# Where weight conversions stand in the queues of ScalarE and VectorE: behind the newest exponential, gh, x and gl

## Chip, cores and metric

One core of a Trainium2 chip runs the whole program. The metric is the device time of one execution in microseconds. The engines meant here are TensorE (PE: matrix products and transposes), ScalarE (ACT), VectorE (DVE) and SyncE (SP, which only issues DMAs). Each works through its own queue in the order in which the program was laid out, and waits on semaphores for what another engine or a DMA has to finish.

## What is computed

Attention with a window of 32 positions for 4 x 512 local queries and full attention for 4 x 32 global ones (8 heads of 64), then two feed-forward layers over the 2176 resulting rows, in float32. The weights come as float64 and are read as raw pairs of int32.

```
out_g = np.matmul(sm(s_g), v_all)                  # s_g: global queries against all keys
s_ll = np.where(mask, s_ll, -1000000000.0)         # mask: |i - j| <= 32
a_l = sm(np.concatenate([s_lg, s_ll], axis=-1))
out_l = np.matmul(a_l, np.concatenate([v_g, v_l], axis=2))
x = rows of concatenate([out_g, out_l])            # 2176 x 512
h = x @ w_in;  g = np.maximum(0.01 * h, h);  x = g @ w_out      # first layer, d_ff 2048
h = x @ w_in2; g = h - np.tanh(h);           out = g @ w_out2   # second layer
```

## The kernel before

**Precision.** Each float32 operand of a large product is split into a high part (written by ScalarE: xh, gh, woh, win) and a low remainder (written by VectorE as a difference: xl, gl, wol, win), and each product is three matmuls.

**Items.** The first layer is worked in 80 items n. An item is a chunk c of up to 512 rows (five chunks, in the order 0, 1, 0, 2, 3, 4; the first and third each with half of the 16 slices) and a slice f of 128 of the 2048 hidden columns. `mlp1_a` does 12 matmuls into the one PSUM bank h, then `mlp1_g` the PReLU g and the high part gh on ScalarE (L206, L207) and the low part gl on VectorE (L208). The next item's h can start when g has read the bank. Two items later `mlp1_b` adds the slice's contribution to four banks y0 to y3 (12 matmuls); after a chunk's last slice `mlp1_y` evicts them through the tile yst (ScalarE L255 for y1 and y3, VectorE L257 for y0 and y2). TensorE's order for this part is written out by hand.

**Attention beside it.** The rest of the attention is worked in stages between the steps of items 0 to 7, 24 to 31, 32 to 47 and 48 to 58. A stage transposes keys and queries (kps, qps, copied to kt, qt by ScalarE), forms scores (sps), takes row minima (VectorE L418 or L412), exponentials e (ScalarE L425), their reciprocal sums and products (VectorE L434, L435, L444), transposes of the probabilities (ptps, copied to pt), and the product with v (avps), whose high part xh ScalarE writes (L485) and whose low part xl VectorE writes (L487). For global queries there are sgps, gtps, gt2ps and gavps. In the run phase all these share three PSUM banks in rotation, so that a transpose can wait for the xl that still has to read the bank.

**Weight conversions.** `convert_w` turns a raw tile (128 x 512 float64) into float32: ScalarE scales the upper words (L128, into wf or w2f), VectorE puts bits together in three steps (L129, L133, L136). First-layer weights are then split (ScalarE L142, VectorE L143) and, for w_out, stored to DRAM (wod); second-layer weights are stored as they are (w2id, w2od) through the tile w2f, which has two buffers. Raw tiles (wraw) have two buffers also; `job_load` issues the load of the next one when a conversion gives its buffer back. `job` is traced at the start of an item: in items 17 to 24 each item has one first-layer conversion, and every second item one of the second layer too; later there is about one second-layer conversion in two items.

**What sets the order.** The scheduler lays out each engine's queue by priority and by when it expects operands. `tc.issue_after(x)` adds an order edge behind instruction x, for instructions on x's engine alone. Before the change first-layer conversions stood behind the newest exponential (ScalarE) and the newest xl (VectorE), second-layer ones behind the newest gl (VectorE) and nothing on ScalarE.

Of the kernel before, what the change touches and what calls it, by code (L numbers as in the profile page):

```python
# [10 lines left out]
AF = mybir.ActivationFunctionType  # L11
# [10 lines left out]
def kernel(  # L22
# [14 lines left out]
    nc = tc.nc  # L37
# [57 lines left out]
    def f32(t):  # L95
        return t.bitcast(F32)
# [21 lines left out]
    def convert_w(raw, w=None):  # L118
        hw, lw = raw[:, :, 1], raw[:, :, 0]
        t = mlp.tile([128, DM], I32, tag="wt", name="wt", bufs=1)  # L120
        if w is None:
            w = mlp.tile([128, DM], F32, tag="wf", name="wf", bufs=2)
        nw[0] += 1

        nc.scalar.activation(w, hw.bitcast(F32), AF.Copy, scale=REBIAS)  # L128
        nc.vector.tensor_scalar(  # L129
            out=t, in0=w.bitcast(I32), scalar1=3, scalar2=0x7FFFFFFF,  # L130
            op0=ALU.logical_shift_left, op1=ALU.bitwise_and,
        )
        nc.vector.scalar_tensor_tensor(  # L133
            out=t, in0=hw, scalar=-0x80000000, in1=t, op0=ALU.bitwise_and, op1=ALU.bitwise_or
        )
        nc.vector.scalar_tensor_tensor(  # L136
            out=w.bitcast(I32), in0=lw, scalar=29, in1=t, op0=ALU.logical_shift_right, op1=ALU.bitwise_or
        )
        return w
# [10 lines left out]
    def wo_split(f, w):  # L150
        hi = mlp.tile([128, DM], F32R, tag="woh", name="woh", bufs=4)
        lo = mlp.tile([128, DM], F32R, tag="wol", name="wol", bufs=3)
        split_w(w, hi, lo, nc.vector)
        wo_t[f] = hi, lo
# [8 lines left out]

    g_t = {}
    y_ps = {}
    anchor = [None]
    last_av = [None]
    last_exp = [None]
    last_kq = [None]
# [14 lines left out]
    def mlp1_a(c, f):  # L184
        N = sizes[c]
        b, n0 = place[c]
        x_h, x_l = xh[b][:, :, n0 : n0 + N], xl[b][:, :, n0 : n0 + N]
        h = []

        def part(d):  # L190
            assert all(p in av_n for p in range(starts[c]//HALF*NP, (starts[c] + 256*halves[c])//HALF*NP) if p % NP == d), (c, f, d)
            if d == 0:
                h.append(bank("h", "h"))
            for i, (w, x) in enumerate(((win_h, x_h), (win_l, x_h), (win_h, x_l))):
                mm(h[0][:, :N], w[f][:, d, :], x[:, d, :], d == 0 and i == 0, d == ND - 1 and i == 2)
            if d == ND - 1:
                mlp1_g(c, f, h[0])

        return [lambda d=d: part(d) for d in range(ND)]

    def mlp1_g(c, f, h):
        N = sizes[c]
        g = mlp.tile([128, 512], F32, tag="g", name="g", bufs=1)
        gh = mlp.tile([128, 512], F32R, tag="gh", name="gh", bufs=3)
        gl = mlp.tile([128, 512], F32R, tag="gl", name="gl", bufs=3)
        nc.scalar.activation(g[:, :N], h[:, :N], AF.Prelu, alpha=0.01)  # L206
        nc.scalar.activation(gh[:, :N], g[:, :N], AF.Copy)  # L207
        anchor[0] = nc.vector.tensor_sub(gl[:, :N], g[:, :N], f32(gh)[:, :N])  # L208
        g_t[c, f] = gh, gl

# [499 lines left out]
            with tc.issue_after(last_kq[0].ins):  # L710
                in_raw.append((f, load_w("in", w1_in, f, place)))

    def converted(raw):


        with tc.issue_after(last_av[0].ins), tc.issue_after(last_exp[0].ins):
            return convert_w(raw)

    def in_job():
        if in_raw:  # L720
            f, raw = in_raw.pop(0)
            w = converted(raw)
            t = win_tile(f)
            split_w(w, t[:, 0], t[:, 1], nc.vector)
# [5 lines left out]
    def job_load():  # L730
        if jobs:
            kind, w, f = jobs.pop(0)
            raws.append((kind, w, f, load_w(kind, w, f)))

    def job():
        kind, src, f, raw = raws.pop(0)
        if src is w1_out:
            wo_split(f, converted(raw))
            hi, lo = wo_t[f]

            def store():
                nc.sync.dma_start(out=wo_dram[f][:, 0], in_=f32(hi))
                nc.sync.dma_start(out=wo_dram[f][:, 1], in_=f32(lo))

        else:
            dst = (w2i_dram if kind == "in" else w2o_dram)[f]
            w = att.tile([128, DM], F32, tag="w2f", name="w2f", bufs=2)
            with tc.issue_after(anchor[0].ins):
                convert_w(raw, w)

            def store():
                nc.sync.dma_start(out=dst, in_=w)

        later.append(store)
        job_load()
# [114 lines left out]
    if True:  # L870
# [58 lines left out]
        for n in range(len(items) + 8):  # L929
            ph, c, f = items[n] if n < len(items) else (3, 0, 0)  # L930
            one = items[n - 1] if 0 < n <= len(items) else (3, 0, 0)
            if ph == 1:
                if n in (0, 2, 4, 6) or HF <= n < 2 * HF:
                    in_job()
                if n in (0, 2) or 4 <= n < 12:
                    in_load()
                for _ in range(job_at.get(n, 0)):
                    job()
                if n == 3 * HF + 1:
                    y_part()  # L940
                if c == 4 and f == 0:
                    while gtodo:
                        gtodo.pop(0)()
                    assert not raws and not jobs
                    att_ctx.close()
                    p2 = ctx.enter_context(tc.tile_pool(name="p2", bufs=1))
                    for k in range(NF - 1):
                        wo2_t.append([p2.tile([128, ND, 128], F32R, name=f"wo2{x}{k}") for x in "hl"])
                    wo2_t.append([x[1][:, :, 512:] for x in (xh, xl)])
                    x2_load(0, 0)  # L950
                    x2_load(0, 1)
                if c == 4:
                    w2_fetched = [fetch2(w2o_dram[f]), fetch2(w2i_dram[f])]
                    if 2 <= f < 2 + ND:
                        x2_split(0, f - 2)
            elif ph == 2 and order2.index(c) + 1 < 5:
                nx = order2[order2.index(c) + 1]
                if f in (2, 3):
                    x2_load(nx, f - 2)
                if 5 <= f < 5 + ND:  # L960
                    x2_split(nx, f - 5)
# [69 lines left out]
```

## Time and profile before

| what | value |
| --- | --- |
| median of 3 runs | 953.87 us (952.01 to 955.35) |
| the profiled execution's own time | 950.58 us |
| its span, first to last instruction | 948.7 us |
| TensorE busy | 918.8 us, 97% of the span |
| VectorE busy | 626.1 us, 66% |
| ScalarE busy | 536.7 us, 57% |
| mean granted TensorE clock | 0.998 of 2.4 GHz |

All times of instructions below are microseconds from the span's start. A row of the timeline gives an instruction's start and duration, and in brackets how long its engine sat idle ahead of it and what released it. The attention's start runs until about 75 us, the first layer until about 590 us, the second from there to the end.

### The profile page before, as it was taken

How to read it: one execution, taken by the hardware profiler on the slowest of the kernel's cores; microseconds unless marked ns; L12 is line 12 of the kernel's file. 1: busy time of each engine (PE TensorE's matmuls, PEld its weight loads, DVE VectorE, ACT ScalarE, POOL GpSimd, SP SyncE). 2: the span in 40 equal slices, each digit the busy share in tenths (PEclk: the TensorE clock that was granted, in tenths of full speed). 3: DMA queues.
4: the chain of work that ended last, by engine and by line, in shares of the span. 5: the costliest groups of instructions: out<-in, count | busy, mean ns of one | idle time of the engine just before them, and what ended most of it. 6: DMA issues, size and time to landing. Idle time of an engine off the chain costs nothing.

```text
span 948.7 us, 15403 instructions
## 1 busy us (share of the span) xinstructions
PE 918.8 (97%) x5436; PEld 769.0 (81%) x5436; DVE 626.1 (66%) x1373; ACT 536.7 (57%) x1223; POOL 37.1 (4%) x67
## 2 busy tenths in 40 slices
PE   7889999998999989999999999999999999999998
PEld 4667778877777878878889998888888888899997
DVE  3877877665535444644232348878888888878886
ACT  5887775344555455554333447555656655555565
POOL 5400000000000000000000000000000000000022
PEclk9999999999999999999999999999999999999999
DMA  7776798478866766665556674001100100010010
GB/s 189 200 193 175 215 309 266 163 245 267 253 180 182 243 183 198 199 197 178 175 181 211 209 245 136 0 1 34 45 1 1 67 1 1 1 45 1 1 34 23
DMA packets 146573, 129.21 MB, mean 136 GB/s; under 512 B 89280, under 2 KB 108736, under 8 KB 146496
## 3 DMA queue, kind: packets, MB, share of 16 engines
q1 hardware_dynamic: 143840, 127.57, 44.7%
q10 hardware_dynamic: 2656, 0.66, 0.3%
q8 instruction: 43, 0.70, 0.3%
q14 instruction: 34, 0.28, 0.1%
HBM read 101.45 MB, written 26.74 MB: 135 GB/s over the span
## 4 chain that ended last, share of the span: by engine, by line
PE 77%; DMA 11%; ACT 5%; DVE 5%; issue 2%; SPq 1%; POOL 0%; ACTq 0%; DVEq 0%
PE h L55 34%; PE o L55 20%; PE y L55 14%; PE sps L55 2%; DMA wraw<-in_moe_w_out_dram 2%; DMA wf<-w2od 2%; PE ptps L455 2%; DMA w2id<-w2f 2%; PE avps L55 2%; DMA w2od<-w2f 2%; ACT e L425 2%; PE sgps L55 1%; PE gavps L55 1%; DVE wt L133 1%; DMA wod<-wol 1%
## 5 line engine op out<-in xcount | busy, mean ns | idle before, releaser
L55 PE MATMUL h<-xh,win 128*128 128x512 f32 (+2 forms) x1280 | 357.3, 362 | 4.3 <-ACT g L206 4.2
L55 PEld LDWEIGHTS h<-xh,win 128*128 128x128 f32 x1280 | 229.0, 189 | 40.7 <-ACT g L206 6.6
L55 PE MATMUL h<-xl,win 128*128 128x512 f32 (+2 forms) x640 | 229.2, 358 | 0.0
L55 PEld LDWEIGHTS h<-xl,win 128*128 128x128 f32 x640 | 120.7, 189 | 15.3
L55 PE MATMUL y<-gh,woh 128*128 128x512 f32 (+2 forms) x320 | 120.9, 378 | 0.0
L55 PE MATMUL y<-gh,wol 128*128 128x512 f32 (+2 forms) x320 | 114.7, 359 | 0.0
L55 PE MATMUL y<-gl,woh 128*128 128x512 f32 (+2 forms) x320 | 114.1, 360 | 0.0
L208 DVE TENSOR_TENSOR gl<-g,gh 128x512 fp32r<-128x512 f32 (+2 forms) x80 | 48.8, 610 | 89.4 <-ACT gh L207 83.2
L55 PE MATMUL o<-wo2l,gh 128*128 128x512 f32 x255 | 99.6, 391 | 0.0
L55 PE MATMUL o<-wo2h,gh 128*128 128x512 f32 x255 | 99.4, 390 | 0.0
L55 PE MATMUL o<-wo2h,gl 128*128 128x512 f32 x255 | 97.7, 390 | 0.0
L635 ACT ACTIVATE u<-h 128x512 f32<-128x512 f32 (+2 forms) x80 | 42.6, 533 | 93.2 <-PE h L55 86.3
L206 ACT ACTIVATE g<-h 128x512 f32<-128x512 f32 (+2 forms) x80 | 42.2, 528 | 50.3 <-PE h L55 49.6
L55 PEld LDWEIGHTS y<-gh,woh 128*128 128x128 f32 x320 | 60.5, 189 | 11.3 <-issue 4.8
L660 ACT ACTIVATE gh<-p 128x512 fp32r<-128x512 f32 (+2 forms) x80 | 45.4, 568 | 41.0 <-DVE p L644 41.0
L55 PEld LDWEIGHTS y<-gl,woh 128*128 128x128 f32 x320 | 60.4, 189 | 7.9
L55 PEld LDWEIGHTS y<-gh,wol 128*128 128x128 f32 x320 | 60.6, 189 | 6.1
L128 ACT ACTIVATE w2f<-wraw 128x512 f32<-128x512 f32 x32 | 21.3, 664 | 71.1 <-DMA w2od<-w2f 30.4
L641 ACT ACTIVATE u<-u,consts 128x512 f32<-128x512 f32 (+2 forms) x80 | 52.7, 659 | 6.8 <-DVE p L639 4.0
L661 DVE TENSOR_TENSOR gl<-p,gh 128x512 fp32r<-128x512 f32 (+1 forms) x64 | 41.9, 654 | 21.9 <-ACT gh L660 21.8
L55 PEld LDWEIGHTS o<-wo2h,gl 128*128 128x128 f32 x255 | 47.9, 188 | 10.1
L55 PEld LDWEIGHTS o<-wo2h,gh 128*128 128x128 f32 x255 | 47.9, 188 | 9.1
(112 smaller groups left out, 1434.0 us busy)
## 6 DMA issues: line engine op xcount, KB each, us to landing
wraw<-in_moe_w_out_dram SPq DMA_DIRECT2D x32, 512.0 KB, 5.2
woh<-wod SPq DMA_DIRECT2D x64, 256.0 KB, 3.7
wol<-wod SPq DMA_DIRECT2D x64, 256.0 KB, 3.2
inraw<-in_moe_w_in_dram SPq DMA_DIRECT2D x16, 512.0 KB, 5.8
wraw<-in_moe_w_in_dram SPq DMA_DIRECT2D x16, 512.0 KB, 5.4
vr<-in_v_l_dram SPq DMA_DIRECT2D x48, 96.0 KB, 3.1
kr<-in_k_l_dram SPq DMA_DIRECT2D x47, 96.0 KB, 3.0
vn<-in_v_l_dram SPq DMA_DIRECT2D x32, 128.0 KB, 3.3
```

The costliest lines, as they stand in the source:

```text
L55: nc.tensor.matmul(o, lhsT, rhs, start=start, stop=stop)
L128: nc.scalar.activation(w, hw.bitcast(F32), AF.Copy, scale=REBIAS)
L133: nc.vector.scalar_tensor_tensor(out=t, in0=hw, scalar=-0x80000000, in1=t, op0=ALU.bitwise_and, op1=ALU.bitwise_or)
L206: nc.scalar.activation(g[:, :N], h[:, :N], AF.Prelu, alpha=0.01)
L208: anchor[0] = nc.vector.tensor_sub(gl[:, :N], g[:, :N], f32(gh)[:, :N])
L425: last_exp[0] = nc.scalar.activation(e[:, h, j, s0 : s0 + n], x, AF.Exp, bias=st[:, k : k + 1], scale=-1.0, accum_out=st[:, 4 + k : 5 + k],)
L455: nc.tensor.transpose(ps[:, k * 128 : (k + 1) * 128], e[:, h, j, c0 : c0 + 128], ident)
L635: nc.scalar.activation(u, h, AF.Square)
L641: nc.scalar.activation(u, u, AF.Square, bias=tc_a2)
L660: nc.scalar.activation(gh[:, :N], p, AF.Copy)
L661: eng["pool" if i == order2[-1] else "dve"].tensor_sub(gl[:, :N], p, f32(gh)[:, :N])
```

## The change

Every conversion, of either layer, now goes through `converted`, which puts ScalarE's part behind the newest exponential and the newest gh, and VectorE's part behind the newest xl and the newest gl that were traced so far.

```diff
-    anchor = [None]
+    anchor, anchor_s = [None], [None]
...
-        nc.scalar.activation(gh[:, :N], g[:, :N], AF.Copy)
+        anchor_s[0] = nc.scalar.activation(gh[:, :N], g[:, :N], AF.Copy)
         anchor[0] = nc.vector.tensor_sub(gl[:, :N], g[:, :N], f32(gh)[:, :N])
...
-    def converted(raw):
-
-
-        with tc.issue_after(last_av[0].ins), tc.issue_after(last_exp[0].ins):
-            return convert_w(raw)
+
+
+    def converted(raw, w=None):
+        with ExitStack() as behind:
+            for x in (last_av, last_exp, anchor, anchor_s):
+                if x[0] is not None:
+                    behind.enter_context(tc.issue_after(x[0].ins))
+            return convert_w(raw, w)
...
-            with tc.issue_after(anchor[0].ins):
-                convert_w(raw, w)
+            converted(raw, w)
```

The instructions are the same in number on every engine, and TensorE's order is the same row for row. Three places show what moves. Buffer numbers stand behind the names here.

ScalarE in the dense stretch, before the change, from the conversions of item 18 to g of item 19 (g_2586 belongs to item 17, g_2639 to 18, g_2685 to 19; wf_2607 and w2f_2618 are item 18's conversions, wf_2661 item 19's):

```order
L128 ACTIVATE wf_2607<-wraw_2527 128x512
L128 ACTIVATE w2f_2618<-wraw_2571 128x512
L142 ACTIVATE woh_2612<-wf_2607 128x512
L206 ACTIVATE g_2586<-h_2573 128x512
L207 ACTIVATE gh_2587<-g_2586 128x512
L128 ACTIVATE wf_2661<-wraw_2616 128x512
L206 ACTIVATE g_2639<-h_2626 128x512
L207 ACTIVATE gh_2640<-g_2639 128x512
L142 ACTIVATE woh_2666<-wf_2661 128x512
```

The same conversions after the change:

```order
L206 ACTIVATE g_2586<-h_2573 128x512
L207 ACTIVATE gh_2587<-g_2586 128x512
L128 ACTIVATE wf_2607<-wraw_2527 128x512
L128 ACTIVATE w2f_2618<-wraw_2571 128x512
L142 ACTIVATE woh_2612<-wf_2607 128x512
L206 ACTIVATE g_2639<-h_2626 128x512
L207 ACTIVATE gh_2640<-g_2639 128x512
L128 ACTIVATE wf_2661<-wraw_2616 128x512
L142 ACTIVATE woh_2666<-wf_2661 128x512
L206 ACTIVATE g_2685<-h_2672 128x512
```

Each item's conversions moved one item later, behind gh of the item ahead, and the split copy of a single conversion (woh_2666) now stands ahead of the next g instead of behind a gh.

VectorE at the same place, before (wt is the bit work's scratch tile; gl_2588 belongs to item 17, gl_2641 to 18):

```order
L143 TENSOR_TENSOR wol_2613<-wf_2607,woh_2612 128x512
L208 TENSOR_TENSOR gl_2588<-g_2586,gh_2587 128x512
L129 TENSOR_SCALAR wt_2619<-w2f_2618 128x512
L133 SCALAR_TENSOR_TENSOR wt_2619<-wraw_2571,wt_2619 128x512
L136 SCALAR_TENSOR_TENSOR w2f_2618<-wraw_2571,wt_2619 128x512
L129 TENSOR_SCALAR wt_2660<-wf_2661 128x512
```

And after:

```order
L208 TENSOR_TENSOR gl_2588<-g_2586,gh_2587 128x512
L129 TENSOR_SCALAR wt_2606<-wf_2607 128x512
L133 SCALAR_TENSOR_TENSOR wt_2606<-wraw_2527,wt_2606 128x512
L136 SCALAR_TENSOR_TENSOR wf_2607<-wraw_2527,wt_2606 128x512
L129 TENSOR_SCALAR wt_2619<-w2f_2618 128x512
L133 SCALAR_TENSOR_TENSOR wt_2619<-wraw_2571,wt_2619 128x512
L143 TENSOR_TENSOR wol_2613<-wf_2607,woh_2612 128x512
L136 SCALAR_TENSOR_TENSOR w2f_2618<-wraw_2571,wt_2619 128x512
L208 TENSOR_TENSOR gl_2641<-g_2639,gh_2640 128x512
```

Second-layer bit work (w2f_2618) stays behind gl_2588; first-layer bit work (wf_2607) moved from ahead of it to behind it.

ScalarE in the attention, items 37 and 38, before (g_4075 is item 37's g, g_4143 item 38's; e1 are the exponentials of the stage between them):

```order
L369 ACTIVATE qt_4099<-qps_4096 128x256
L425 ACTIVATE e1_134,st_4122<-e1_134,st_4122 128x192
L425 ACTIVATE e1_134,st_4122<-e1_134,st_4122 128x224
L128 ACTIVATE w2f_4373<-wraw_4049 128x512
L425 ACTIVATE e1_134,st_4122<-e1_134,st_4122 128x192
L206 ACTIVATE g_4143<-h_4109 128x256
L425 ACTIVATE e1_134,st_4122<-e1_134,st_4122 128x224
L485 ACTIVATE xh512_67<-avps_4152 128x256
L207 ACTIVATE gh_4144<-g_4143 128x256
```

And after:

```order
L369 ACTIVATE qt_4099<-qps_4096 128x256
L425 ACTIVATE e1_134,st_4122<-e1_134,st_4122 128x192
L425 ACTIVATE e1_134,st_4122<-e1_134,st_4122 128x224
L425 ACTIVATE e1_134,st_4122<-e1_134,st_4122 128x192
L206 ACTIVATE g_4143<-h_4109 128x256
L425 ACTIVATE e1_134,st_4122<-e1_134,st_4122 128x224
L207 ACTIVATE gh_4144<-g_4143 128x256
L485 ACTIVATE xh512_67<-avps_4152 128x256
L128 ACTIVATE w2f_4200<-wraw_3880 128x512
```

The scaling left the exponentials; an older one (w2f_4200, which stood among the exponentials of the stage ahead) now stands behind xh. On VectorE gl_4145 and the four products of e moved from behind xl to ahead of it at this place.

ScalarE at the end of chunk 0's first half, before (yst from y1 and y3 are the evictions; g_2262 is item 10's g):

```order
L142 ACTIVATE win10_2236<-wf_2231 128x512
L207 ACTIVATE gh_2200<-g_2199 128x512
L255 ACTIVATE yst_2220<-y1_1321 128x512
L128 ACTIVATE wf_2336<-inraw12_2099 128x512
L128 ACTIVATE w2f_2388<-wraw_2180 128x512
L142 ACTIVATE win11_2286<-wf_2281 128x512
L255 ACTIVATE yst_2226<-y3_1323 128x512
L206 ACTIVATE g_2262<-h_2249 128x512
```

And after:

```order
L207 ACTIVATE gh_2200<-g_2199 128x512
L128 ACTIVATE wf_2231<-inraw10_1892 128x512
L255 ACTIVATE yst_2220<-y1_1321 128x512
L142 ACTIVATE win10_2236<-wf_2231 128x512
L206 ACTIVATE g_2262<-h_2249 128x512
L207 ACTIVATE gh_2263<-g_2262 128x512
L128 ACTIVATE wf_2281<-inraw11_2021 128x512
L128 ACTIVATE w2f_2291<-wraw_2111 128x512
L255 ACTIVATE yst_2226<-y3_1323 128x512
```

The eviction of y3 moved from ahead of g of item 10 to behind its gh and two scalings.

## Rows read from the trace of the kernel before

**Rows 1.** Busy time by engine, whole span.
```profile
PE 918.8 (97%) x5436; PEld 769.0 (81%) x5436; DVE 626.1 (66%) x1373; ACT 536.7 (57%) x1223; POOL 37.1 (4%) x67
```
**Rows 2.** Waits of TensorE: for whom, us in total, times, longest.
```profile
PE gt2ps L576 <- DVE xl L487: 5.4, 3, 2.9
PE h L55 <- ACT g L206: 4.2, 4, 1.6
...
PE ptps L455 <- DVE xl L487: 3.1, 5, 1.2
```
**Rows 3.** ScalarE's groups: busy, mean ns, idle before, releasers.
```profile
L128 ACT ACTIVATE w2f<-wraw 128x512 f32<-128x512 f32 x32 | 21.3, 664 | 71.1 <-DMA w2od<-w2f 30.4 <-DMA w2id<-w2f 23.7 <-DMA wraw<-in_moe_w_out_dram 10.2
```
**Rows 4.** Timeline of TensorE, instructions that it stood idle for.
```profile
210.78 0.73 PE L55 MATMUL h<-xh,win 128*128 128x512 f32 x2 [1.13 <-ACT g L206]
...
223.54 0.73 PE L55 MATMUL h<-xh,win 128*128 128x512 f32 x2 [1.57 <-ACT g L206]
...
241.14 0.97 PE L55 MATMUL sps<-kt,qt 64*128 64x192 f32 x6 [0.33 <-ACT kt L358]
...
344.95 0.28 PE L576 MATMUL gt2ps<-ident,sg 128*32 128x128 f32 x1 [2.92 <-DVE xl L487]
...
408.32 0.28 PE L576 MATMUL gt2ps<-ident,sg 128*32 128x128 f32 x1 [1.96 <-DVE xl L487]
```
**Rows 5.** Chain of work that ended last, around 182 us.
```profile
182.45 2.72 PE h L55 x12
```
**Rows 6.** Timeline of ScalarE in the dense stretch.
```profile
199.47 0.67 ACT L128 ACTIVATE wf<-wraw 128x512 f32<-128x512 f32 x1 [0.88 <-DMA wraw<-in_moe_w_out_dram]
...
209.07 0.66 ACT L128 ACTIVATE w2f<-wraw 128x512 f32<-128x512 f32 x1 [3.24 <-DMA wraw<-in_moe_w_in_dram]
...
210.15 0.58 ACT L206 ACTIVATE g<-h 128x512 f32<-128x512 f32 x1
...
221.83 0.66 ACT L128 ACTIVATE w2f<-wraw 128x512 f32<-128x512 f32 x1 [3.17 <-DMA wraw<-in_moe_w_out_dram]
...
240.07 0.66 ACT L128 ACTIVATE w2f<-wraw 128x512 f32<-128x512 f32 x1 [2.91 <-DMA wraw<-in_moe_w_out_dram]
```
**Rows 7.** Timeline of VectorE in the dense stretch.
```profile
212.03 0.42 DVE L129 TENSOR_SCALAR wt<-w2f 128x512 int32<-128x512 int32 x1
...
215.20 0.69 DVE L136 SCALAR_TENSOR_TENSOR wf<-wraw,wt 128x512 int32<-128x512 int32 x1
```
**Rows 8.** Timeline of SyncE in the dense stretch: raw loads issued.
```profile
195.75 0.33 SPq L113 DMA_DIRECT2D wraw<-in_moe_w_out_dram  x1
...
215.96 0.33 SPq L113 DMA_DIRECT2D wraw<-in_moe_w_out_dram  x1
...
233.21 0.34 SPq L113 DMA_DIRECT2D wraw<-in_moe_w_out_dram  x1
```
**Rows 9.** Timeline around the stall at 345 us.
```profile
342.34 0.66 ACT L128 ACTIVATE w2f<-wraw 128x512 f32<-128x512 f32 x1 [2.08 <-DMA w2id<-w2f]
342.90 0.44 ACT L425 ACTIVATE e<-e,st 128x192 f32<-128x192 f32 x1
...
344.50 0.40 DVE L487 TENSOR_TENSOR xl<-avps,xh 128x256 fp32r<-128x256 f32 x1
344.81 1.03 DVE L444 TENSOR_SCALAR e<-e,st 128x192 f32<-128x192 f32 x4
```
**Rows 10.** Timeline around the stall at 408 us.
```profile
401.12 0.08 DVE L418 DVE_READ_ACCUMULATOR2_ANT st<- 128x1 f32 x1
...
402.71 0.66 ACT L128 ACTIVATE w2f<-wraw 128x512 f32<-128x512 f32 x1 [2.61 <-DMA w2od<-w2f]
```
**Rows 11.** Stretch behind the stall at 345 us: busy times, granted clock.
```profile
345.00:349.00 4.00, 4.00 (x22) 4.00 (x23) 2.90 (x8) 1.49 (x4) 0.00 (x0) 0.57 0.09 16
```
**Rows 12.** Timeline of ScalarE and TensorE at the eviction of y3.
```profile
158.60 0.60 ACT L255 ACTIVATE yst<-y 128x512 f32<-128x512 f32 x1 [0.50 <-DMA yp<-yst]
...
159.83 0.39 PE L55 MATMUL y<-gh,woh 128*128 128x512 f32 x1
```

## The prediction

> **What bounds the kernel now.** I read the table of busy time first, then TensorE's waits, then each of these waits in the timeline together with what stands in ScalarE's and VectorE's queues at that moment. TensorE is busy for 97% of the span [rows 1], so the most a reordering on the other engines can return is TensorE's idle time, and of that only the part that lies where orders change: between about 75 and 500 us. There TensorE waits for few things [rows 2]: for g (4.2 us, the PReLU that frees the one bank of h), for xl before a transpose into a bank that xl has to read out first (gt2ps 5.4 us, ptps 3.1 us). The second half of the program has no wait of TensorE that the change could touch.
>
> The causes sit one step further back. ScalarE's scaling of raw weights (L128 into w2f) made its queue idle for 71.1 us, nearly all of it for DMAs: the store that must leave the w2f buffer first (30.4 and 23.7) or the raw tile itself (10.2) [rows 3]. ScalarE works its queue in order, so whatever stands behind such a scaling waits too, and when this is an exponential or g, TensorE is next.
>
> The reader should see three kinds of place:
>
> *Dense stretch, 195 to 241 us* (items 17 to 24, three conversions in two items). Three of the four waits for g fall here, 4.0 of their 4.2 us (two of them, 1.13 and 1.57 us, in rows 4), and 0.33 us for kt [rows 4]: 4.3 us. The 12 matmuls of h take 2.72 us [rows 5], the 12 of y as long, so two items without a wait are 10.88 us; here the scaling at 209.07 comes back at 221.83, 12.76 us later [rows 6]. The loop that does this: scaling of the second-layer tile on ScalarE ahead of g; g, gh; gl on VectorE; only then the bit work of that tile, as it was queued behind gl, and behind this the bit work of the next single tile, 212.03 to 215.89 [rows 7]; with it a raw buffer comes free and the load goes out at 215.96 [rows 8], landing 5.87 us later [rows 6].
>
> *Scalings between exponentials, 300 to 410 us.* The scaling at 342.34 stands between two exponentials and has kept the queue idle for 2.08 us; the third exponential starts at 342.90, xl at 344.50 [rows 9], and TensorE stands still for 2.92 us [rows 4]. At 402.71 the same, 2.61 us, ahead of all four exponentials [rows 10], then 1.96 us on TensorE [rows 4]. After the 2.92 us the granted clock fell: 0.57 on average from 345 to 349 [rows 11], that is mostly the lower level, 1.2 GHz; 4 x 0.43 = 1.7 us of work lost. After 1.96 us it did not fall.
>
> *Eviction of y, 150 to 160 us.* No wait before, but a close one: the last eviction (y3) ran 158.60 to 159.20, TensorE's first matmul into that bank started at 159.83 [rows 12].
>
> **The change, part by part.** No instruction is added or removed; TensorE's order does not change, and SyncE's is nearly the same. What moves is listed in the order blocks above.
>
> *Scalings between exponentials: taken out.* Each second-layer scaling now stands behind gh of the item ahead, one to three items later than before, while its bit work keeps its place on VectorE (behind gl). So the raw loads and the w2f stores go out when they did, and the scaling meets data that landed long ago: the 54 us of waiting for stores should nearly vanish from ScalarE. For the stall at 344.95: ScalarE fell idle at 342.34 - 2.08 = 340.26, and there the third exponential can start, 2.65 us earlier; all behind it follows. VectorE's new order costs something: gl and the four products of e (1.03 [rows 9], 1.3 with gl) now stand ahead of xl, which so starts at 344.50 - 2.65 + 1.3 = 343.15 and ends 0.4 later. TensorE ran dry at 344.95 - 2.92 = 342.03, so 1.5 us of wait stay and 1.35 are gained. At 408.32 the exponentials can start when the first row maximum is out, at 401.20 [rows 10], not behind the scaling at 403.27: 2.05 us earlier; xl ended just ahead of 408.32, with one ready scaling and gl ahead of it in both orders, and I take 0.3 off for their places: 1.75 gained, 0.2 of wait left. Three of the five waits of ptps, at 359, 370 and 381 us (together 1.2 of the 3.1 in rows 2), have only that cause and go. The longest, 1.2 at 323 us, hangs on y evictions; VectorE gets 0.3 shorter ahead of it. The rest of gt2ps's 5.4 us, 0.57 at 307 us, goes, as two pieces of bit work leave the row maxima. If no second stall replaces the one at 344.95, the clock stays up: 1.7. Sum here 1.35 + 1.75 + 1.2 + 0.3 + 0.6 + 1.7 = 6.9 us; bounds 3 (clock loss stays, xl later than worked out) and 8.5 (all waits gone).
>
> On the clock, "TensorE: Matmul & The Clock Gate" of the Trainium skill (What's actually happening) says that the throttled state is the default and activity releases it, and that the transition moves from run to run; by it the 1.7 us could be missing from other executions, and the sum would be 1.7 us smaller. The rows agree on the two levels; which runs have the drop no row of one execution shows.
>
> *Dense stretch: the loop gets shorter.* Scaling and bit work of a tile now stand behind the same item's gh and gl, so g, gh, gl and the queue behind them leave the loop. What is left is each raw buffer's own cycle. With scaling 0.66 and bit work 1.9 from end to end [rows 6, 7] a single tile gives its buffer back 2.6 us after its scaling starts; a second-layer tile takes 3.2, because the copy of the lower part (wol) comes in ahead of its last step. Loads took 3.72 us alone (195.75 to 199.47) and 5.87 beside another [rows 6, 8]. Three conversions on one buffer, the middle of them loaded beside another: 2.6 + 5.9 + 3.2 + 4.0 + 2.6 + 4.0 = 22.3 us, against four items, 21.8. So g gets late by 0.5 us per four items, 1 to 2 us over the stretch with a little contention. It may: the g that started at 210.15 cost 1.13 us, so one at 209.0 costs nothing, 2.1 us after the last matmul of h. What is late next is not g but kt: the pair of item 24 and its split copy now stand ahead of kt and qt. With each scaling at the later of two times, gh ahead of it or its load, I get scalings at 197.4 and 198.6 (item 18), 204.0, 208.6 and 212.5, 215.7, 220.2 and 223.9, 227.1, 231.6 and 235.8 (item 24). Bit work, split copy, kt and qt behind the last one end near 237.9. The scores are due at 241.14 - 0.33 - 4.0 = 236.8 [rows 4], so they wait about 1.1 us. In the old order a scaling at 240.07 did the same on a smaller scale [rows 6]. The stretch keeps 1.1 of 4.3 us: 3.2 gained; bounds 4.3 (loads at 3.7) and -1 (a microsecond more per load).
>
> For the load, "DMA: Bandwidth & Descriptors" of the Trainium skill (Anatomy of one DMA) gives about 2.0 us and bytes over 436 GB/s, 3.2 us for these 512 KB, fitted on another queue's path; by it no score would wait and the sum would be 1.1 us larger. Rows 6 and 8 show 3.72 at best, and they decide.
>
> *Eviction of y: a loss.* The last eviction on ScalarE now stands behind gh of item 10 and two scalings instead of ahead of g. g can start when h is done, nine matmuls of 2.72 / 12 ahead of 159.83, near 157.9; gh ends at 159.1, two scalings take 0.55 each, the eviction lasts until 160.8; TensorE wants the bank at 159.83. About 1.0 us lost; bounds 0 and 2 (if the store of the buffer it writes is late as well).
>
> *Sum.* 6.9 + 3.2 - 1.0 = 9.1 us off the profiled execution: 950.6 - 9.1 = 941.5. The median of the runs, 953.87, lies 3.3 us above that execution; I take the same 9.1 us off it: 944.8.
>
> **The rivals.**
> 1. *Only part of it.* The dense stretch stays as bad as it was, because the raw buffers' cycle and not the loop over g binds it. For it: 22.3 against 21.8 has no room. Against it: the 12.76 us loop is longer than either buffer's cycle. Gain 6.9 - 1.0 = 5.9 or, with the clock loss kept, 4.2 us: 948 to 950.
> 2. *No change.* The stalls move: 0.95 us more ahead of each xl, 0.55 ahead of copies of pt and kt behind gh, at some ten places each in which TensorE has no wait today. At 0.5 us in a dozen places 6 us are gone: 951 to 955. Against it: between 410 and 575 us, where the same scalings stood between copies, TensorE waited 0.2 us in all.
> 3. *Slower.* The split copy of a single tile now stands ahead of g; before it stood behind gh. So g waits for load, scaling, bit work and copy in a row. If loads take 6.9 us each (233.21 to 240.07 is one such [rows 6, 8]), the cycle is 8.4 + 3 x 6.9 = 29.1 us per four items, 7.3 too long, twice, less the 2.1 us that g may be late: 12.5 us of stall in place of 4.3. With 5.9 gained elsewhere that is 2.3 us slower, 956; more if the clock falls in the longer stalls. It decides from about 6.5 us per load on. The lone loads of 3.72 speak against it.
>
> **How the numbers follow.** Forecast (6 to 11.5 us gained) 0.60; still more gained (the scores' wait and the rest of the xl waits gone too) 0.06; rival 1 0.16; rival 2 0.11; rival 3 0.07. A measurement of this kernel tells about 0.3% (2.9 us) from no change. Faster by more than that: 0.60 + 0.06 + most of rival 1 = 0.80; within 0.12; slower 0.08. The likeliest time is 944.8; its own range is 942.5 to 948. The range that holds eight in ten takes in 11 to 13 us gained at one end and rival 1 at the other: 941.5 to 951.
>
> **What would show it.** In the changed kernel's waits, the w2f scalings should wait less than 20 us for stores, the wait of h for g should be under 1 us, gt2ps under 3 us. New waits should be y (for the eviction of y3, near 160 us, about 1 us) and sps for kt near 237 us (1 to 2 us). The clock near 345 us should stay at 1.00. The prediction is wrong if g still stalls TensorE three times around 210 to 236 us, if new waits of ptps or sps appear between 320 and 500 us, or if MLP2 (from 600 us) changes.

## The result, and the profile after

| what | before | after |
| --- | --- | --- |
| median | 954.19 us (952.01 to 955.35, 4 runs) | 943.13 us (942.62 to 943.91, 4 runs) |
| ratio, 95% interval | | 0.9887 [0.9868, 0.9907] |
| profiled execution: own time, span | 950.58, 948.7 | 943.49, 941.7 |

The change makes the kernel faster by 1.1%. The time lies inside the range, 1.7 us under the forecast of 944.8. The same kernel was timed again beside the experiments below: 942.97 us against 951.01 there, 0.9912 [0.9893, 0.9931].

I read the views of after in the order of before. TensorE's busy time hardly changed (918.8 us before [rows 1]), as its work is the same:

```profile
PE 917.3 (97%) x5436; PEld 768.1 (82%) x5436; DVE 627.2 (67%) x1373; ACT 536.7 (57%) x1223; POOL 36.9 (4%) x67
```

TensorE's waits (for whom, us in total, times, longest), to be held against [rows 2]. The wait for g fell from 4.2 to 0.7, that of gt2ps from 5.4 to 2.6; two waits for y and one for kt are new or longer.

```profile
PE gt2ps L576 <- DVE xl L487: 2.6, 3, 1.5
...
PE ptps L455 <- DVE xl L487: 2.1, 2, 1.4
...
PE y L55 <- ACT yst L255: 0.8, 1, 0.8
...
PE h L55 <- ACT g L206: 0.7, 2, 0.4
PE sps L55 <- ACT kt L358: 0.6, 1, 0.6
PE y L55 <- DVE yst L257: 0.4, 1, 0.4
```

ScalarE's group of second-layer scalings (busy, mean ns, idle before, releasers). The 54.1 us of waiting for stores [rows 3] are gone; what is left is 7.4 us for raw tiles.

```profile
L128 ACT ACTIVATE w2f<-wraw 128x512 f32<-128x512 f32 x32 | 21.1, 659 | 7.4 <-DMA wraw<-in_moe_w_in_dram 4.4 <-DMA wraw<-in_moe_w_out_dram 3.0
```

Timeline of TensorE after, the instructions that it stood idle for (start, duration; idle time in brackets). The first is there to set the clocks of the two traces against each other; in the trace of before it started at 114.70 after the same wait of 0.68.

```profile
116.16 0.33 PE L455 MATMUL ptps<-ident,e 128*128 128x128 f32 x1 [0.68 <-DVE xl L487]
...
161.00 0.50 PE L55 MATMUL y<-gh,woh 128*128 128x512 f32 x1 [0.42 <-DVE yst L257]
...
162.79 0.50 PE L55 MATMUL y<-gh,woh 128*128 128x512 f32 x1 [0.83 <-ACT yst L255]
...
239.58 0.46 PE L55 MATMUL sps<-kt,qt 64*128 64x192 f32 x2 [0.59 <-ACT kt L358]
...
305.15 0.28 PE L576 MATMUL gt2ps<-ident,sg 128*32 128x128 f32 x1 [0.72 <-DVE xl L487]
...
321.89 0.33 PE L455 MATMUL ptps<-ident,e 128*128 128x128 f32 x1 [1.38 <-DVE xl L487]
...
341.78 0.28 PE L576 MATMUL gt2ps<-ident,sg 128*32 128x128 f32 x1 [1.49 <-DVE xl L487]
...
400.12 0.29 PE L576 MATMUL gt2ps<-ident,sg 128*32 128x128 f32 x1 [0.41 <-DVE xl L487]
...
513.84 0.44 PE L55 MATMUL h<-xh,win 128*128 128x384 f32 x1 [0.44 <-ACT g L206]
```

TensorE's order is the same in both kernels, so the start of one and the same matmul can be compared in two traces. Five of them cut the program into places (114.70, 159.83, 241.14, 344.95 and 408.32 of before, [rows 4, 12]), and the difference from one to the next is what a place gained or lost. For after: +1.46, then +1.50 more (y), -4.52 (dense stretch), -1.61 and -5.03 (scalings between exponentials, 6.64 together), and +1.2 from there to the end, at 941.7 for 948.7. That is 7.0 us between the two profiled executions.

The first +1.46 comes ahead of every moved wait. The windows of after (PE busy, then PEld, DVE, ACT, POOL; granted clock as the third figure from the end) show it: here the clock fell near 65 us, and not behind the stall at 341.8. Before, it was the other way round [rows 11], and 64.5 to 68.5 us had 1.00. In a second profiled execution of the changed kernel (e8 below) the clock stayed up there, and the same matmul stands at +0.42; so about 1.0 us of the 1.46 went with the clock.

```profile
64.50:68.50 4.00, 4.00 (x33) 2.95 (x33) 2.05 (x11) 2.14 (x7) 0.00 (x0) 0.57 0.71 160
...
345.00:349.00 4.00, 4.00 (x45) 3.51 (x42) 0.64 (x3) 1.98 (x6) 0.00 (x0) 1.00 0.77 210
```

The place at 341 us, timeline of ScalarE and VectorE (compare [rows 9]). The first exponential waits 1.85 us for the row minima, as it did before; the third now follows behind it 0.92 us later and waits for nothing. The scaling stands behind xh; on VectorE gl and the four products of e stand ahead of xl.

```profile
337.50 0.46 ACT L425 ACTIVATE e<-e,st 128x192 f32<-128x192 f32 x1 [1.85 <-DVE st L418]
...
338.42 0.44 ACT L425 ACTIVATE e<-e,st 128x192 f32<-128x192 f32 x1
...
340.15 0.65 ACT L128 ACTIVATE w2f<-wraw 128x512 f32<-128x512 f32 x1
...
340.02 0.42 DVE L208 TENSOR_TENSOR gl<-g,gh 128x256 fp32r<-128x256 f32 x1
340.36 1.03 DVE L444 TENSOR_SCALAR e<-e,st 128x192 f32<-128x192 f32 x4
341.31 0.41 DVE L487 TENSOR_TENSOR xl<-avps,xh 128x256 fp32r<-128x256 f32 x1
```

The end of chunk 0's first half, SyncE's queue and ScalarE's eviction of y3 in after. The store of y1 is among the three at 157.50, behind two weight fetches. Two things make the eviction late. ScalarE, behind g and gh of item 10, is through with the second scaling only at 161.63 (160.97 + 0.66); then the eviction waits 0.51 us more for a store to land. TensorE, 1.46 us behind the trace of before, would have come to this bank near 161.3 (159.83 + 1.46, an estimate). So the place in the queue alone makes the eviction, which takes 0.60, end about 0.9 us late, and the store adds 0.51.

```profile
154.62 0.38 SPq L113 DMA_DIRECT2D wraw<-in_moe_w_in_dram  x1
155.05 0.50 SPq L754 DMA_DIRECT2D w2id<-w2f  x1
155.64 0.38 SPq L259 DMA_DIRECT2D yp<-yst  x1
156.30 0.32 SPq L160 DMA_DIRECT2D wol<-wod  x1
156.71 0.69 SPq L159 DMA_DIRECT2D woh<-wod  x1
157.50 5.58 SPq L259 DMA_DIRECT2D yp<-yst  x3
...
160.97 0.66 ACT L128 ACTIVATE w2f<-wraw 128x512 f32<-128x512 f32 x1
162.14 0.60 ACT L255 ACTIVATE yst<-y 128x512 f32<-128x512 f32 x1 [0.51 <-DMA yp<-yst]
```

### The profile page after: what moved, and what is told of

Read it like the earlier page. It is cut to its first block, busy times and chain, and to the rows that moved or that the text cites. A ratio compares the mean times of both kernels' runs of the same rounds, so it can differ in the third digit from the quotient of the medians.

```text
span 941.7 us, 15410 instructions
## 1 busy us (share of the span) xinstructions
PE 917.3 (97%) x5436; PEld 768.1 (82%) x5436; DVE 627.2 (67%) x1373; ACT 536.7 (57%) x1223; POOL 36.9 (4%) x67
## 4 chain that ended last, share of the span: by engine, by line
PE 81%; DMA 7%; DVE 5%; ACT 5%; issue 2%; SPq 0%; POOL 0%; ACTq 0%; DVEq 0%
PE h L55 34%; PE o L55 20%; PE y L55 15%; DMA wf<-w2od 4%; PE sps L55 3%; PE avps L55 3%; PE ptps L455 2%; ACT e L425 1%; DMA wraw<-in_moe_w_out_dram 1%; PE sgps L55 1%; PE gavps L55 1%; DVE wt L133 1%; PE kps L356 1%; DVE wf L136 1%; PE qps L365 1%
## 5 line engine op out<-in xcount | busy, mean ns | idle before, releaser
L425 ACT ACTIVATE e<-e,st 128x224 f32<-128x224 f32 (+1 forms) x88 | 40.2, 458 | 29.1 <-DVE st L418 29.1
```

Source lines behind the costliest of these rows:

```text
L425: last_exp[0] = nc.scalar.activation(e[:, h, j, s0 : s0 + n], x, AF.Exp, bias=st[:, k : k + 1], scale=-1.0, accum_out=st[:, 4 + k : 5 + k],)
```

## The experiments

My theory when the first were sent (theory A) was that three places add up: scalings taken from between exponentials, the shorter loop of the dense stretch, and y's eviction, where I read the trace after as a late store and not the place forecast. The rivals stand in the expectations.

The table shows, for the profiled execution of each kernel, by how many us the same matmul starts later (+) or earlier (-) than before the change, and the change of the span.

```
kernel                 114.70  159.83  241.14  344.95  408.32    span
after                    1.46    2.96   -1.56   -3.17   -8.20   -7.0
e1 second layer only     1.48    1.52   -4.05   -6.28  -11.30  -11.3
e2 first layer only      0.43    1.95   -2.67   -3.66   -4.38   -4.1
e3 ScalarE only          1.88    3.40   -1.61   -0.13   -5.06   -2.6
e4 VectorE only          1.47    4.41    2.01    3.67    2.07    2.2
e5 no store wait         6.82   14.08   11.97   13.76   12.53   12.3
e6 store of y1 first     0.23    1.94   -2.51   -4.14   -9.17   -7.4
e7 xl first              0.82    0.78   -4.81   -8.50  -13.53  -12.4
e8 changed again         0.42    1.96   -1.47   -1.41   -6.44   -5.8
e9 items 8 to 10         1.68    1.71   -3.05   -4.54   -9.56   -9.4
e10 late splits         -0.61   -0.52   -6.10   -9.76  -14.79  -12.4
```

**e1, second layer only.**

```diff
-            for x in (last_av, last_exp, anchor, anchor_s):
+            for x in (last_av, last_exp) if w is None else (last_av, last_exp, anchor, anchor_s):
```

> Only second-layer conversions go behind the newest exponential, gh, x and gl; first-layer conversions stand as before the change. Theory A (three places that add up: scalings between exponentials 6.6 us gained, loop of the dense stretch 4.6 us gained, eviction of y 1.75 us lost because y1's store is queued behind two weight fetches on SyncE): attention's gain is whole, the dense stretch keeps most of its gain since the second-layer scaling leaves its place ahead of g, and y loses nothing because y1's store stands ahead of the fetches again; about 1.5 us faster than the changed kernel, 941.5. Theory B (the dense stretch gains because first-layer bit work and scalings moved): the stretch stays at 3 to 4 us of waits for g, about 945.5.

Measured 939.19 us (938.16 to 940.25), 0.9863 [0.9843, 0.9882]. The places of the attention gain 7.2 us, y loses nothing (1.52 - 1.48), and the dense stretch gains 5.6 us, more than in the changed kernel: no wait for g and none for kt is left between 195 and 245 us. ScalarE in that stretch (timeline): the second-layer scaling stands behind gh, and the split copy of a first-layer tile (215.41) behind a gh as well, where the changed kernel has it ahead of g.

```profile
209.49 0.63 ACT L207 ACTIVATE gh<-g 128x512 fp32r<-128x512 f32 x1
210.03 0.66 ACT L128 ACTIVATE w2f<-wraw 128x512 f32<-128x512 f32 x1
...
214.55 0.63 ACT L207 ACTIVATE gh<-g 128x512 fp32r<-128x512 f32 x1
215.41 0.63 ACT L142 ACTIVATE woh<-wf 128x512 fp32r<-128x512 f32 x1 [0.23 <-DVE wf L136]
```

So the second-layer half alone is enough for all of the gain, and no loss at y comes without the first-layer half. Theory B falls.

**e2, first layer only.**

```diff
-            for x in (last_av, last_exp, anchor, anchor_s):
+            for x in (last_av, last_exp, anchor, anchor_s) if w is None else (anchor,):
```

> Only first-layer conversions go behind the newest exponential, gh, x and gl; second-layer ones stand behind the newest gl on VectorE alone, as before the change. Theory A: the waits for xl between 340 and 410 us are all back (2.9, 0.3, 0.2, 0.7, 2.0), the dense stretch gains some 4.5 us, y loses 1.7 us since y1's store stands behind two weight fetches as in the changed kernel: 2.8 us faster than before, 951.4. If y was lost by the two scalings ahead of the last eviction and not by the store, one scaling is gone from there and the wait of y for ScalarE is shorter by some 0.5 us. Theory B gives the dense stretch the same 4.5 us; the two differ in the other run.

Measured 950.82 us (946.55 to 954.67), 0.999 [0.997, 1.001]: no change that can be told (the profiled execution, 4.1 us ahead in the table, was the quickest of its runs). TensorE's waits (as above): xl is back with 4.5 and 2.7 us, and y waits as in the changed kernel, 0.9 and 0.4. Between gh and the eviction of y3 there is one scaling fewer, but ScalarE is not free any sooner for that: the other one stands ahead of g of item 10, waits 1.01 us for a store there, starts at 158.44, and g starts at 159.01 behind it. So this run does not tell the eviction's place from the stores. The dense stretch gains 4.6 us, as in the changed kernel, so there either half is enough.

```profile
PE gt2ps L576 <- DVE xl L487: 4.5, 3, 2.2
...
PE ptps L455 <- DVE xl L487: 2.7, 4, 1.1
...
PE y L55 <- ACT yst L255: 0.9, 1, 0.9
```

**e3, ScalarE only, and e4, VectorE only.**

```diff
-            for x in (last_av, last_exp, anchor, anchor_s):
+            for x in (last_exp, anchor_s, last_av if w is None else anchor):           # e3
+            for x in (last_av, anchor) + ((last_exp,) if w is None else ()):           # e4
```

> ScalarE's part of every conversion is ordered as in the changed kernel, VectorE's part as before the change (first layer behind the newest xl, second behind the newest gl). Theory A: ScalarE's scalings are what held the exponentials and g up, and VectorE's bit work follows them by itself: same time as the changed kernel, 943.1 within 1 us. Rival: VectorE's edges carry part of the dense stretch's gain (bit work of a first-layer tile no longer ahead of gl): 945 or more.

> VectorE's part of every conversion is ordered as in the changed kernel, ScalarE's as before the change (first layer behind the newest exponential, second behind nothing). Theory A: scalings stand between exponentials again and wait for stores there, so none of the 6.6 us of the attention comes back; in the dense stretch the scaling of a second-layer tile mostly stands behind gh in this order too, so 3 to 4 us are gained there; y loses 1 to 2 us: 951 to 953. Rival (VectorE's edges carry the gain): 947 or less.

e3 measured 944.07 us (941.95 to 947.91), 0.9918 [0.9897, 0.9939], and e4 955.37 us (953.11 to 961.77), 1.0035 [1.0017, 1.0053]: ScalarE's edges are the change, VectorE's alone make the kernel a little slower. In e4, which was expected at 951 to 953, the place between exponentials gains nothing (+0.1 from 241 to 408), the dense stretch gains 2.4 us where 3 to 4 were expected (5.0 in e3), and y loses 2.9 us. e3 can't be told from the changed kernel by time, but its trace shows what VectorE's edges were good for: in six places xl stands one to three rows further back. The timeline of VectorE in e3 shows one of them, where a step of bit work is ahead of xl; TensorE's wait behind it was 1.71 us instead of 1.38, and the clock fell after it.

```profile
321.60 1.03 DVE L444 TENSOR_SCALAR e<-e,st 128x224 f32<-128x224 f32 x4
322.55 0.42 DVE L129 TENSOR_SCALAR wt<-w2f 128x512 int32<-128x512 int32 x1
322.88 0.42 DVE L487 TENSOR_TENSOR xl<-avps,xh 128x256 fp32r<-128x256 f32 x1
```

**e5, no store wait** (the kernel before, with the edit shown).

```diff
-                nc.sync.dma_start(out=dst, in_=w)
+                nc.sync.dma_start(out=dst, in_=f32(flat(win_h[0])))
```

> The kernel before the change, but the stores of second-layer weights send another finished tile of the same size, so that no scaling has to wait for a store (the converted second-layer weights are thus never stored, and the second layer works with other numbers). The same DMAs run. Theory A (the attention lost its time to scalings that waited for stores while exponentials stood behind them): the stalls at 345 and 408 us shrink from 2.9 and 2.0 to under 1.5 and 0.5 though the scaling still stands ahead of the exponentials, some 4 to 5 us; in the dense stretch, where the scaling waits for its raw tile, the three waits for g stay at about 4 us in all: 947.5. Rival (the scaling's place and the order of VectorE's row maxima, products and xl cost the time, not the store): the stalls stay and the time is that of before, 952.

Measured 963.83 us (961.16 to 965.1), 1.013 [1.0105, 1.0154], against both expectations. The scheduler no longer saw a store to wait for, and its order changed in places (counted by the gh ahead of them, six of the 32 scalings stand one item earlier and three one later); now they wait for raw tiles, 60.6 us in all (group of ScalarE, columns as above).

```profile
L128 ACT ACTIVATE w2f<-wraw 128x512 f32<-128x512 f32 x32 | 21.3, 665 | 60.6 <-DMA wraw<-in_moe_w_out_dram 33.2 <-DMA wraw<-in_moe_w_in_dram 27.4
```

The one ahead of the exponentials waited 3.04 us (timeline of ScalarE).

```profile
353.53 0.67 ACT L128 ACTIVATE w2f<-wraw 128x512 f32<-128x512 f32 x1 [3.04 <-DMA wraw<-in_moe_w_in_dram]
354.10 0.44 ACT L425 ACTIVATE e<-e,st 128x192 f32<-128x192 f32 x1
```

TensorE then stood still for 3.57 us at 358.71, 2.92 before. So the store was only what the scaling happened to wait for; with another DMA in its place the stall is no shorter. From 241 to 408 us this kernel neither gains nor loses much (+0.6); what it lost lies ahead of 160 us (6.82 and 7.26 in the table), where the clock fell near 69 us for 6.8 us and near 162 us for 3.4, and y waited 2.5 us for a converted weight and 2.8 for an eviction. Since order and loads changed too, this run doesn't price the store by itself.

**e6, store of y1 first** (the changed kernel; two weight fetches are held until y1 is stored).

```diff
+                last_y[0] = nc.sync.dma_start(out=to[:, d, :N], in_=st[:, :N])
+                if d == 1 and c == 0 and f < NF - 1:
+                    while held:
+                        with tc.issue_after(last_y[0].ins):
+                            wo_fetch(held.pop(0))
...
+                if n in (HF, HF + 1):
+                    held.append(fetches.pop(0))
```

> The changed kernel with one thing put back: the store of y1 is issued ahead of the two weight fetches that stand between y0's and y1's store on SyncE. ScalarE's order is that of the changed kernel, with the eviction of y3 behind g, gh and two scalings. Theory A (the eviction waits for the landing of y1's store, 162.12, as its own wait of 0.51 us says): TensorE's second wait for y falls from 0.83 to 0.4 us or less, the rest being the two scalings. Theory C, that of the prediction (the eviction's place behind gh and two scalings costs the time): 0.83 stays. The total moves by half a microsecond only and is read from the trace.

Measured 943.41 us (943.19 to 943.85), 0.9919 [0.9899, 0.994]. ScalarE's order is that of the changed kernel. The wait of TensorE for y3 is gone although the eviction stands behind gh and two scalings; it starts at 160.48, right behind them (the edit moves lines: L257 and L259 here are L255 and L257 of the other kernels):

```profile
159.76 0.64 ACT L128 ACTIVATE w2f<-wraw 128x512 f32<-128x512 f32 x1
160.48 0.60 ACT L257 ACTIVATE yst<-y 128x512 f32<-128x512 f32 x1
```

That does not refute theory C, because another wait hid this one: the wait for y2, which VectorE evicts, rose to 1.6 us (waits of TensorE), as VectorE could evict it only at 160.22, when the store of y0, issued at 154.43, had landed. TensorE so came to y3 only at 161.77 (159.83 + 1.94 in the table), when its eviction had ended (160.48 + 0.60 = 161.08). Without the wait for y2 it would have come near 160.06 (159.83 + 0.23, an estimate), and the eviction would have been 1.0 us late by its place alone. The stretch lost 1.71 us, 1.50 in the changed kernel.

```profile
PE y L55 <- DVE yst L259: 1.6, 1, 1.6
```

**e7, xl first** (e1, and the products of e behind the newest xl).

```diff
+    def products(s):
+        with tc.issue_after(last_av[0].ins):
+            smax_b(s)
...
-            ops.append(lambda: (score(s, [tag(), tag()]), smax_a(s), smax_b(s)))
-        ops.append(cols)
+            if s < PRE:
+                ops.append(lambda: (score(s, [tag(), tag()]), smax_a(s), smax_b(s)))
+            else:
+                ops.append(lambda: (score(s, [tag(), tag()]), smax_a(s)))
+        ops.append(cols if s < PRE or s > last else lambda: (cols(), products(s)))
```

> Only second-layer conversions behind the newest exponential, gh, x and gl (as in the first experiment), and in the run phase the four products of e are queued behind xl instead of ahead of it. If, as the prediction worked out, the 1.5 us that is left of the wait for xl at 339 us comes from gl and the products (1.3 us) standing ahead of xl, this wait falls under 0.6 us and the others for xl shrink too: 1.5 to 2.5 us faster than the first experiment, 937. Rival (the exponentials and row maxima themselves come late): the waits for xl stay, or come back as waits of ptps for the products, 939 to 940.

Measured 938.14 us (937.00 to 938.51), 0.9861 [0.9841, 0.9882]. That is 4.8 us under the changed kernel in the same series (e8, 942.97, at least 941.92), the two sets of runs 3.4 us apart; against e1 it is 1.05 us, where 1.5 to 2.5 were expected. TensorE's waits: gt2ps 1.1 us where e1 has 2.6, ptps 0.8 for 2.0; one wait for a row minimum is new.

```profile
PE gt2ps L576 <- DVE xl L487: 1.1, 3, 0.5
...
PE ptps L455 <- DVE xl L487: 0.8, 2, 0.5
...
PE sgps L55 <- DVE st L418: 0.5, 1, 0.5
```

The longest wait fell from 1.50 to 0.55 us, by about the products' 1.03. Of the 2.2 us that its trace is ahead of e1's at 408 us, 1.1 are left at the end; it can't be told from e1 by the ratios.

**e8, the changed kernel again**, unaltered.

> The changed kernel again, unaltered, timed beside the others: 943 within 1.5 us. If the clock falls for 3.4 us near 65 us in this execution too, before any moved instruction, that loss belongs to the execution and not to the change.

942.97 us (941.92 to 944.68). The clock stayed up near 65 us here. It fell near 240 us instead, behind a wait for kt of 1.69 us that was 0.59 in the first trace of the same kernel. ScalarE's row shows why: the raw tile of item 24, whose load was issued at 231.44, let the scaling start at 238.08, 6.6 us later, and kt stands behind it (239.16).

```profile
238.08 0.66 ACT L128 ACTIVATE w2f<-wraw 128x512 f32<-128x512 f32 x1 [3.84 <-DMA wraw<-in_moe_w_in_dram]
```

**e9, items 8 to 10** (the changed kernel).

```diff
+    item = [-1]
...
-            for x in (last_av, last_exp, anchor, anchor_s):
+            for x in (last_av, last_exp) if item[0] in (8, 9, 10) and w is None else (last_av, last_exp, anchor, anchor_s):
```

> The changed kernel, but the first-layer conversions traced in items 8, 9 and 10 (three of the sixteen of w_in) stand as before the change; all others, and all second-layer ones, stay behind the newest exponential, gh, x and gl. Theory D (y's loss is made on the DMA path: bit work that moved behind gl gives its raw and w2f buffers back some 2 us later, so the next raw load and the w2f store go out just ahead of the stores of y0 and y1, and both land late): the loss near 160 us, 1.8 us in all three traces of the changed order, goes to 0.2 or less and nothing else changes: 941.3. Rival (the newest gh ahead of the second-layer scaling of item 9 is enough for the loss, whatever the first layer does): the loss stays above 1 us and the time is that of the changed kernel, 943.

Measured 941.88 us (941.12 to 944.06), 0.9879 [0.9859, 0.99]. The loss near 160 us is gone (1.71 - 1.68), the other places are as in the changed kernel (-4.8 in the dense stretch, -6.5 behind it). SyncE's queue shows the raw load and the store of w2f 2.1 us earlier than in the changed kernel, and both first stores of y ahead of the fetches:

```profile
152.47 0.38 SPq L113 DMA_DIRECT2D wraw<-in_moe_w_in_dram  x1
152.91 0.67 SPq L756 DMA_DIRECT2D w2id<-w2f  x1
155.46 1.07 SPq L259 DMA_DIRECT2D yp<-yst  x2
156.64 0.40 SPq L160 DMA_DIRECT2D wol<-wod  x1
```

That is what theory D says: a load and a store that became possible only when the bit work was done stood ahead of y's stores in SyncE's queue and moved beside them. But the run does not tell it from theory C, since the eviction of y3 went back to its old place on ScalarE too, ahead of g of item 10:

```profile
160.43 0.60 ACT L255 ACTIVATE yst<-y 128x512 f32<-128x512 f32 x1 [4.24 <-DMA yp<-yst]
160.92 0.59 ACT L206 ACTIVATE g<-h 128x512 f32<-128x512 f32 x1
```

It stands ahead of that g in every run without the loss (before, e1, e7, e9, e10) and behind it in every run with the loss. No run moved the place alone, so how much is the place and how much the stores is not shown by an experiment.

**e10, late splits** (e7, and the splits of fetched second-layer weights behind the newest gh).

```diff
     def w2_place(kind, f, t):
+        with tc.issue_after(anchor_s[0].ins):
+            w2_place_(kind, f, t)
```

> The kernel with xl ahead of the products, and also the splits of the fetched second-layer weights in the last 16 items of the first layer (ScalarE copies that wait 1 to 5 us for a fetch, with g behind them) behind the newest gh. If TensorE lost the 0.6 to 1.8 us between 500 and 575 us (traces of the changed order) to g standing behind such a copy, that loss goes to under 0.3: about 1 us faster, 937. Rival: the copies give the two wf buffers back later, the fetches go out later, and the second layer starts later: 1 us or more slower, 939 and above. TensorE's order in the second layer may move a little, since only its first part is written out by hand.

Measured 938.68 us (938.05 to 941.14), 0.9854 [0.9829, 0.9878]: not to be told from e7. Its trace is 14.79 us ahead at 408 us and no wait of TensorE follows until 563 us, so the end of the first layer loses nothing; but two waits of 1.8 us in all open in the second layer, and 2.4 us are given back by the end. The gain was turned into another wait.

```profile
PE h L55 <- DVE t L644: 1.8, 2, 1.1
```

## Why the prediction was right, and where not

*Scalings between exponentials: 6.9 forecast, 6.64 measured.* Of its terms, the stall at 344.95 was to keep 1.5 us and kept 1.49; that at 408.32 was to keep 0.2 and kept 0.41; the three waits of ptps at 359, 370 and 381 us are gone; the clock stayed up there (1.7). The cause is shown from both sides: with ScalarE's edges alone (e3) the scalings leave the exponentials and the waits for stores go, and without the second layer's (e2) or without ScalarE's (e4) the stalls are back (2.19 and 1.76 us in e2, 1.90 and 1.64 in e4). e7 shows that what is left at 341.78 is the products ahead of xl, as the working had it. Two terms failed for the same reason: 0.57 us at 307 and 0.3 of the wait at 323 were to go, but they rose to 0.72 and 1.38. The price of gl and products ahead of xl was put on one stall only, while these two pay it also; in e7, without it, they fall to 0.17 and 0.53 (the 0.41 at 400 us stays there). The three waits of ptps made up for it: taking them away was worth 1.9 us by the start of the same matmuls (from 350 to 382 us), not 1.2. That the sum came out within 0.3 us is partly luck.

*Dense stretch: 3.2 forecast, 4.5 measured.* All three waits for g went, and the wait of sps for kt came as forecast, at 239.58 for "near 237", 0.59 us for 1.1. The working took the rest of the stretch as 4.3 us of waits; the same matmuls show that taking away 4.34 us of waits and adding 0.59 gained 4.52 and not 3.75, so a wait cost some 0.2 us more than its row. Rival 3 named the right risk: in e8 one load of 6.6 us made the kt wait 1.69. But one long load in the stretch is not every load, and on the whole it did not decide. In e1, where the split copy stands behind gh and not ahead of g and kt, the stretch gains 5.6; the other first-layer conversions are back in their old places there too, so that the copy alone makes the difference is likely and not shown.

*Eviction of y: 1.0 lost forecast, 1.50 measured.* The prediction said that the eviction of y3 is late because it stands behind gh of item 10 and two scalings. By the rows this place is worth about 0.9 us, close to the forecast; the other 0.5 is the landing of y1's store, which the prediction named only for its upper bound of 2. The wait of 0.42 for y2, which hangs on the landing of y0's store, it did not have. It called SyncE's order "nearly the same"; that order held the store of y1 behind two fetches, and a raw load behind bit work. The two causes lie side by side: e6, which put the store of y1 first and left the place, lost no less than the changed kernel, by the wait for y2. The shares are worked out from rows, and the stores' part (e9) was not separated from the place by a run.

*What was not in the sum.* From 408 us to the end 1.2 us were given back. The prediction let a gain made at 400 us stand to the end. Between 500 and 575 us g stands behind copies that wait for fetched weights; one such copy waited 5.63 us and g came 0.44 us late (513.84). In e8 0.6 us went there and in e6 1.8, with the same order of these copies, so it changes from execution to execution with the fetches.

*The sum.* 9.1 us forecast; 7.0 between the two profiled executions, from which the clock near 65 us took about 1.0, and 11.1 between the medians of the first series, 8.0 between those of the series of e8. So that the forecast lies 1.7 us from the median is partly luck: the parts were off by 0.3, 1.3 and 0.5 us, 1.2 us were lost at the end, and the medians of before themselves differ by 3.2 us between series. Before the change single runs lie between 947.95 and 956.17 us over all series, after it between 941.92 and 944.68. A part of this spread goes with the clock: of 43 timed runs of before in the experiments' series, the 17 with a mean granted clock of 0.995 or less have a median of 953.2 us, the 11 with 0.998 or more one of 951.5. The rest of the spread is unexplained.

## What to carry to other kernels

An instruction that waits for a DMA belongs behind the work that the busiest engine is about to need, in a queue that is worked in order; which DMA it waits for matters little, as taking away one wait brought the next (e5). Move only those that wait at such a place: here the second layer's conversions alone gained all of it (e1), and moving the first layer's too brought the loss at y. When an order on one engine is changed, read the queue that issues the DMAs too: here a load that could go out only at 154.62 and two fetches stood ahead of y1's store, and its landing added half a microsecond. And when two causes lie side by side, a run that takes one away and gains nothing has not cleared the other (e6).

## What the runs showed of the hardware

The granted clock fell once or more in ten of the twelve profiled executions ahead of their last two microseconds, for 3.4 us each time (once for 6.8, in e5), at places that changed. At the same wait of 2.5 us that ends near 63.5 us it fell in six of the twelve (in after, about 1.0 us went with it) and stayed up in six. Of later stalls it fell at or behind those of 2.92 us (before), 2.19 (e2), 1.71 (e3), 1.69 (e8) and 2.00, 2.48 and 3.57 (e5), and not behind 1.96 (before), 1.90 and 2.67 (e4) or 2.84 (e5), so the length of a stall alone does not tell. "TensorE: Matmul & The Clock Gate" of the Trainium skill (What's actually happening) says that the transition moves from run to run, and these traces agree.

A raw load of 512 KB took from 3.8 us (issued at 226.00 in after) to 6.6 us (e8) in the dense stretch of one and the same program, so a working that rests on one execution's loads, as that of the dense stretch did, is good to a microsecond per place at best.
